# A clustered attention with a max-out feed-forward: the second copy of k's high part made by a DMA within the same partitions instead of by ScalarE

## Chip, cores and metric

The kernel runs on one core of one Trainium2 chip. The metric is the device time of one execution in microseconds (us); the median of three timed runs before the change is 864.36 us (862.89 to 865.15). A profiled execution is a run of its own, with a time of its own.

## What is computed

Attention over 4 batches, 8 heads, 768 tokens and a head dimension of 64, in which a query sees the keys of its own cluster alone, followed by a feed-forward block that takes the maximum of three products.

```python
q_assign = argmax(einsum('bhsd,hcd->bhsc', q_n, c_n), axis=-1)   # 16 clusters
k_assign = argmax(einsum('bhsd,hcd->bhsc', k_n, c_n), axis=-1)
mask = q_assign[:, :, :, None] == k_assign[:, :, None, :]
scores = scale * matmul(q, k.transpose(0, 1, 3, 2))
scores = where(mask, scores, -1e9)
attn = softmax(scores)
x = matmul(attn, v)            # to [3072 tokens, 512]
h = maximum(maximum(x @ w1, x @ w2), x @ w3)     # 512 -> 768
out = h @ w_out                                  # 768 -> 512
```

## The kernel before

**Staging of q and k.** The host hands over q and k of one head side by side, so that a tile `x` of 128 partitions has q's 64 dimensions in partitions 0 to 63 ("up") and k's in 64 to 127 ("dn"), with 768 tokens along the row. Products are made nearly exact by splitting each number into a high part that TensorE's fp32r format holds and a low remainder. For two heads (a pair) there is one tile `qk` of 128 partitions with four slots, `AQ, BQ, BK, AK`, of 2 x 768 numbers each:

- line 363 (ScalarE) writes the high parts of q and k into BQ; line 366 (GpSimd, at a few places VectorE) writes the low parts, `x - BQ`, into AQ.
- `qk_moves` (lines 369 to 376) then brings the parts where the products need them: line 373 (ScalarE) writes the scaled high part of k into AK up; line 374 (ScalarE) writes the same into BK up; line 375 (a DMA) copies k's low part from AQ dn to AK dn; line 376 (GpSimd) overwrites AQ dn with the scaled high part of q, for which line 375 must have read AQ dn.
- the cluster scores (lines 401 to 408, TensorE) and `cluster_rows` (lines 419 to 457, VectorE and GpSimd) yield one-hot rows, and line 452 (four small DMAs) puts them in partitions 64 to 79 of BQ and BK. Where a pair is prepared a second time, line 394 reads them back from a copy in DRAM.

The first pair of the first batch has its own, faster path (`first_k_moves`, lines 379 to 385). All others, 16 calls, go through `qk_moves`. One tile is prepared while the one before is in use (two buffers).

**A step of the attention.** There are 192 steps (4 batches x 8 heads x 6 blocks of 128 queries). In each, line 478 multiplies AQ with AK (128 rows: low q with high k, high q with low k), line 480 adds BQ with BK (80 rows: high with high, and the mask rows) in one of three PSUM buffers `big`. Line 483 (VectorE) takes the row maximum, line 486 (ScalarE) the exponential and its row sum, lines 487 and 488 the reciprocal. The result is normed and split into two halves of fp16, `hl` (three buffers), in one of two ways that a table `BY_POOL` chooses: lines 496 (ScalarE) and 497 (VectorE), in 147 steps, or lines 492 and 494 (GpSimd) with 493 (ScalarE), in 45. Line 498 has a DMA transpose `hl` into `pt`. For each three steps of two heads, line 510 multiplies `pt` with v.

**Around it.** Weights are loaded (line 192) and split (lines 194 to 207) during the first third. The feed-forward block of a batch (lines 545 to 590) is spread over the steps of the next one, and that of the last half batch stands at the end.

**What sets the order.** Each piece of work has a priority by the step at which it is due, and a scheduler sets the order in which each engine's instructions stand; so an edit at one place can reorder work elsewhere. All DMAs are issued by SP, in order: an issue that waits for data holds back all that stand behind it.

Of the kernel before, what the change touches and what calls it, by code (L numbers as in the profile page):

```python
# [14 lines left out]
AF = mybir.ActivationFunctionType  # L15
# [8 lines left out]
def kernel(  # L24
# [23 lines left out]
    nc = tc.nc  # L48
# [296 lines left out]
    AQ, BQ, BK, AK = range(4)  # L345
    SCALE = 1.0 / D**0.5
# [22 lines left out]
    def qk_moves(b, pr):  # L369
        t = qkt[b, pr]  # L370
        x = t.bitcast(F32)
        up, dn = slice(0, D), slice(D, 2 * D)
        nc.scalar.activation(t[up, AK], x[dn, BQ], AF.Copy, scale=SCALE)
        nc.scalar.activation(t[up, BK], x[dn, BQ], AF.Copy, scale=SCALE)
        nc.sync.dma_start(out=x[dn, AK], in_=x[dn, AQ])
        nc.gpsimd.tensor_scalar(t[dn, AQ], x[up, BQ], SCALE, 1.0, op0=ALU.mult, op1=ALU.mult)

# [81 lines left out]
    def prep_units(b, pr, pool, again=False):  # L459
        u = [lambda i=i: qk_prep(b, pr, i, pool, again) for i in range(2)]  # L460
        if again:
            f = [qk_moves, qk_masks, v_prep]
        else:
            f = [cluster_scores, qk_moves, cluster_rows] + [v_prep] * (b > 0)
        u += [lambda g=g: g(b, pr) for g in f]
        return u
# [222 lines left out]
    for b in range(B):  # L689
# [3 lines left out]
        if b:  # L693
            visits += [(b, pr, tuple(range(NG))) for pr in range(NPAIR)]
            for pr in range(NPAIR):
                if (b, pr) > (1, 0):
                    t = at + pr * 2 * V
# [60 lines left out]
```

## Time and profile before

| | |
|---|---|
| median of three timed runs | 864.36 us |
| the profiled execution, its own time | 869.48 us |
| its span, first to last instruction | 867.7 us |
| busy TensorE / VectorE / ScalarE / GpSimd | 724.6 / 604.0 / 515.3 / 487.0 us |
| mean granted TensorE clock | 0.927 |
| DMAs of line 375 | 16, each 384 KB, median 4.6 us from issue to landing |
| transposes of line 498 | 192, median 4.1 us from issue to landing |
| DMA queue of SP | 130.22 MB, 72.0% of the time of 16 engines |

The profile gives busy time per engine and, for the idle time in front of an instruction, the engine and line that ended it. "PE" is TensorE's matmuls, "PEld" its weight loads, "DVE" VectorE, "ACT" ScalarE, "POOL" GpSimd, "SPq" the DMA issues. The chain of waits starts at the last instruction and goes back, at each step to what released it.

### The profile page before, as it was taken

The page shows a single profiled execution, that of the slowest core. Times are in us where ns is not written, and L with a number is a line of the kernel's source. Part 1 is how long each engine was busy: PE and PEld are TensorE (multiplying, and loading weights), DVE is VectorE, ACT ScalarE, POOL GpSimd, SP SyncE. Part 2 cuts the span into 40 slices and gives each one's busy share as a digit, 9 for nine tenths or more (in the row PEclk, how much of TensorE's full clock was granted, in tenths as well). Part 3 has the DMA queues.
Part 4 walks back from the last instruction along what each step waited for, and adds up shares of the span by engine and source line. Part 5 has one row for each costly group of instructions (what it writes and reads, how often), then busy time and mean ns, then how long its engine had stood idle before and what let it go on. Part 6 is the DMA issues. An engine that isn't in the chain of part 4 may idle for free.

```text
span 867.7 us, 12613 instructions
## 1 busy us (share of the span) xinstructions
PE 724.6 (84%) x4220; PEld 447.9 (52%) x4220; DVE 604.0 (70%) x1135; ACT 515.3 (59%) x843; POOL 487.0 (56%) x470
## 2 busy tenths in 40 slices
PE   3534676686877999797989897979999999999997
PEld 2322444354554566464656564645655566556463
DVE  7888977978989868886769775856777677511020
ACT  7674566856957576768676756566766676510101
POOL 4695673655874467667756464746565655312111
PEclk9999666878896999989899998989999999999999
DMA  6765888999968879789798888789797865810000
GB/s 219 202 153 131 175 148 184 212 216 234 230 127 161 186 126 238 150 164 212 130 185 154 181 174 154 133 151 199 125 178 123 171 127 110 154 47 1 37 1 37
DMA packets 327680, 131.02 MB, mean 151 GB/s; under 512 B 304192, under 2 KB 313408, under 8 KB 327616
## 3 DMA queue, kind: packets, MB, share of 16 engines
q1 hardware_dynamic: 327616, 130.22, 72.0%
q8 instruction: 33, 0.54, 0.3%
q14 instruction: 31, 0.25, 0.1%
HBM read 38.57 MB, written 7.08 MB: 53 GB/s over the span
## 4 chain that ended last, share of the span: by engine, by line
PE 28%; DMA 7%; DVE 7%; ACT 5%; POOL 5%; issue 4%; SPq 0%; POOLq 0%; ACTq 0%; DVEq 0%
PE one L545 14%; DMA pt<-hl 6%; PE one L579 6%; PE one L510 3%; POOL hl L494 2%; DVE hl L497 2%; DVE nm L483 2%; PE big L478 2%; ACT hl L496 2%; ACT e L486 2%; PE big L480 1%; DMA stage<-in_v_dram 1%; POOL e L492 1%; DVE onehot L438 1%; ACT qk L363 1%
## 5 line engine op out<-in xcount | busy, mean ns | idle before, releaser
L486 ACT ACTIVATE e<-big,nm 128x768 f32<-128x768 f32 x192 | 171.6, 895 | 109.6 <-DVE nm L483 51.5
L497 DVE SCALAR_TENSOR_TENSOR hl<-e,r,hl 128x768 f16<-128x768 f32 x147 | 196.8, 1345 | 52.7 <-ACT hl L496 46.2
L545 PE MATMUL one<-x,w16a 128*128 128x384 f16 x1152 | 207.4, 336 | 5.5 <-ACT wf_h L555 3.8
L483 DVE TENSOR_REDUCE nm<-big 128x1 f32<-128x768 f32 x192 | 178.6, 946 | 11.8 <-PE big L480 11.2
L478 PE MATMUL big<-qk 128*128 128x512 f32 (+1 forms) x384 | 129.0, 419 | 68.9 <-ACT e L486 54.4
L496 ACT ACTIVATE hl<-e,r 128x768 f16<-128x768 f32 x147 | 136.1, 932 | 76.5 <-DMA pt<-hl 61.9
L545 PEld LDWEIGHTS <-w16a 128*128 128x128 f16 x1152 | 111.2, 100 | 89.1 <-issue 24.4
L510 PE MATMUL one<-pt,v 128*64 128x384 f16 x1152 | 114.8, 350 | 15.2 <-DMA pt<-hl 11.0
L480 PE MATMUL big<-qk 80*128 80x512 f32 (+1 forms) x384 | 114.8, 381 | 13.7 <-DMA qk<-cl_t 11.4
L478 PEld LDWEIGHTS big<-qk 128*128 128x128 f32 x384 | 69.3, 213 | 101.8 <-ACT e L486 71.5
L545 PE MATMUL one<-x,w16b 128*128 128x384 f16 x576 | 104.9, 338 | 7.3 <-DVE vf_h L557 5.9
L510 PEld LDWEIGHTS <-v 128*64 128x64 f16 x1152 | 73.4, 117 | 52.6 <-issue 24.7
L366 POOL TENSOR_TENSOR qk<-stage,qk 128x768 fp32r<-128x768 f32 x32 | 65.1, 2052 | 54.2 <-ACT qk L363 50.8
L494 POOL TENSOR_TENSOR hl<-e,hl 128x768 f16<-128x768 f32 x45 | 76.5, 1707 | 20.7 <-ACT hl L493 17.7
L480 PEld LDWEIGHTS big<-qk 80*128 80x128 f32 x384 | 68.8, 216 | 26.3 <-issue 8.8
L545 PEld LDWEIGHTS <-w16b 128*128 128x128 f16 x576 | 56.3, 101 | 49.6 <-issue 17.9
L487 DVE TENSOR_SCALAR r<-r 128x1 f32<-128x1 f32 x192 | 27.5, 144 | 49.2 <-ACT e L486 48.8
L492 POOL TENSOR_SCALAR e<-e,r 128x768 f32<-128x768 f32 x45 | 45.3, 1009 | 23.9 <-DVE r L488 20.9
L557 DVE SCALAR_TENSOR_TENSOR wf_h<-one,wf_h 128x384 f32<-128x384 f32 x48 | 26.5, 552 | 46.3 <-PE one L545 46.0
L557 DVE SCALAR_TENSOR_TENSOR vf_h<-one,vf_h 128x384 f32<-128x384 f32 x48 | 26.4, 550 | 46.2 <-PE one L545 46.2
L563 POOL TENSOR_SCALAR wf_h<-wf_h 128x384 f16<-128x384 f32 x24 | 16.2, 676 | 69.3 <-DVE wf_h L557 55.0
L579 PE MATMUL one<-wo,vf_h 128*128 128x512 f16 x216 | 50.2, 389 | 0.8 <-ACT o L588 0.8
(128 smaller groups left out, 934.7 us busy)
## 6 DMA issues: line engine op xcount, KB each, us to landing
stage<-in_qk_dram SPq DMA_DIRECT2D x36, 384.0 KB, 4.1
stage<-in_v_dram SPq DMA_DIRECT2D x25, 384.0 KB, 4.4
wd<-in_moe_w_dram SPq DMA_DIRECT2D x18, 512.0 KB, 4.6
qk<-qk SPq DMA_DIRECT2D x16, 384.0 KB, 4.6
out_dram<-o SPq DMA_DIRECT2D x24, 256.0 KB, 2.7
pt<-hl SPq DMA_TRANSPOSE x192, 4.1
wd<-in_moe_w_out_dram SPq DMA_DIRECT2D x6, 512.0 KB, 4.8
qk<-cl_t SPq DMA_DIRECT2D x56, 48.0 KB, 2.1
```

Source lines behind the costliest of these rows:

```text
L366: last["lo"] = eng.tensor_tensor(t[:, AQ, i], x, t[:, BQ, i].bitcast(F32), op=ALU.subtract)
L478: nc.tensor.matmul(t[:, lo:hi], aq[:, qs], ak[:, lo:hi], start=True, stop=False)
L480: last["pe"] = nc.tensor.matmul(t[:, lo:hi], bq[0:K2, qs], bk[0:K2, lo:hi], start=False, stop=True)
L483: last["nm"] = nc.vector.tensor_reduce(nm, e, axis=AX.X, op=ALU.max, negate=True)
L486: nc.scalar.activation(x, e, AF.Exp, bias=nm, scale=1.0, accum_out=r)
L492: nc.gpsimd.tensor_scalar(x, x, r, 1.0, op0=ALU.mult, op1=ALU.mult)
L494: nc.gpsimd.tensor_tensor(hl[:, 1, :], x, hl[:, 0, :], op=ALU.subtract)
L496: nc.scalar.activation(hl[:, 0, :], x, AF.Copy, scale=r)
L497: nc.vector.scalar_tensor_tensor(hl[:, 1, :], x, r, hl[:, 0, :], op0=ALU.mult, op1=ALU.subtract)
L510: nc.tensor.matmul(t[D * i : D * i + D, 0:NB], v[:, i, kt, va], pt[i][:, :, pa * QT + kt, :], start=(n == 0), stop=(n == len(todo) - 1),)
L545: nc.tensor.matmul(t[:, 0:NB], w16[jt // JA][:, jt % JA, wa, i, ct], x16[b, gi, ct][:, xa, :], start=(n == 0), stop=(n == 3 * CT - 1),)
L579: nc.tensor.matmul(t[:, 0:DM], h16[jt][:, ha, tt * P : (tt + 1) * P], wo16[0][:, jt, wa, :], start=(n == 0), stop=(n == 3 * JT - 1),)
```

## The change

Line 374 no longer computes. In its place SP issues a DMA that copies AK up, which line 373 has just written, to BK up: 64 partitions, 2 x 768 fp32 each, source and destination in the same partitions.

```diff
 def qk_moves(b, pr):
     t = qkt[b, pr]
     x = t.bitcast(F32)
     up, dn = slice(0, D), slice(D, 2 * D)
     nc.scalar.activation(t[up, AK], x[dn, BQ], AF.Copy, scale=SCALE)
-    nc.scalar.activation(t[up, BK], x[dn, BQ], AF.Copy, scale=SCALE)
+    nc.sync.dma_start(out=x[up, BK], in_=x[up, AK])
     nc.sync.dma_start(out=x[dn, AK], in_=x[dn, AQ])
     nc.gpsimd.tensor_scalar(t[dn, AQ], x[up, BQ], SCALE, 1.0, op0=ALU.mult, op1=ALU.mult)
```

The scheduler sets the order of all engines anew. At three places it reads as follows.

ScalarE, at the preparation of the second pair of the third batch (the tenth of the 16 calls); before:

```order
L363 CAST qk<-stage 128x768 x2
L496 ACTIVATE hl<-e,r 128x768
L373 ACTIVATE qk<-qk 64x1536
L374 ACTIVATE qk<-qk 64x1536
L496 ACTIVATE hl<-e,r 128x768
L486 ACTIVATE e,r<-big,nm 128x768
```

and now:

```order
L363 CAST qk<-stage 128x768 x2
L496 ACTIVATE hl<-e,r 128x768
L373 ACTIVATE qk<-qk 64x1536
L496 ACTIVATE hl<-e,r 128x768
L486 ACTIVATE e,r<-big,nm 128x768
L496 ACTIVATE hl<-e,r 128x768
```

One instruction is gone, and the rest keeps its order here.

SP's queue at the same call; before:

```order
L330 DMA stage<-in_v_dram 128x768
L498 DMA_TRANSPOSE pt<-hl 128x12x128
L375 DMA qk<-qk 64x1536
L353 DMA stage<-in_qk_dram 128x768
L498 DMA_TRANSPOSE pt<-hl 128x12x128 x2
L353 DMA stage<-in_qk_dram 128x768
L498 DMA_TRANSPOSE pt<-hl 128x12x128 x5
L452 DMA qk<-cl_t 16x768 x4
```

and now:

```order
L330 DMA stage<-in_v_dram 128x768
L498 DMA_TRANSPOSE pt<-hl 128x12x128
L374 DMA qk<-qk 64x1536
L375 DMA qk<-qk 64x1536
L498 DMA_TRANSPOSE pt<-hl 128x12x128 x3
L353 DMA stage<-in_qk_dram 128x768 x2
L498 DMA_TRANSPOSE pt<-hl 128x12x128 x3
L452 DMA qk<-cl_t 16x768 x4
```

The new DMA stands right ahead of line 375, and the two loads of the next q and k come behind three transposes. In 13 of the 16 calls the new DMA is ahead of line 375, in three behind it.

GpSimd, at the first two of the 16 calls, near the start of the program; before:

```order
L448 TENSOR_SCALAR qk<-cl_t 16x768 x2
L376 TENSOR_SCALAR qk<-qk 64x1536
L366 TENSOR_TENSOR qk<-stage,qk 128x768 x2
L430 TENSOR_TENSOR cl_t<-cl_t 128x24x16
L492 TENSOR_SCALAR e<-e,r 128x768
```

and now:

```order
L448 TENSOR_SCALAR qk<-cl_t 16x768 x2
L366 TENSOR_TENSOR qk<-stage,qk 128x768
L376 TENSOR_SCALAR qk<-qk 64x1536
L430 TENSOR_TENSOR cl_t<-cl_t 128x24x16
L366 TENSOR_TENSOR qk<-stage,qk 128x768
L492 TENSOR_SCALAR e<-e,r 128x768
```

Line 376, which waits for the DMA of line 375, has moved behind the first low part of the next pair.

## The prediction

> **What bounds the kernel now.** I read the busy time by stretches first, then the chain of waits that ended last, then the waits by engine, and last the places where the moved copy stands. In the stretches the columns are length, then busy time of PE, PEld, DVE, ACT and POOL with instruction counts, the granted TensorE clock, the DMA share and GB/s.
>
> ```profile
> 0.00:300.00 300.00, 197.18 (x952) 125.11 (x953) 256.36 (x476) 197.64 (x316) 192.63 (x203) 0.85 0.83 186
> 300.00:768.00 468.00, 433.28 (x2729) 270.00 (x2727) 334.21 (x636) 307.41 (x508) 275.89 (x241) 0.96 0.80 158
> 768.00:867.00 99.00, 94.13 (x544) 52.76 (x540) 13.38 (x24) 10.27 (x19) 18.47 (x26) 1.00 0.04 17
> ```
>
> There are three regimes. Up to 300 us VectorE is the fullest engine (256.36 of 300 us, 85%) and the DMA engines are 83% busy. From 300 to 768 us TensorE works 433.28 of 468 us, so at most 34.7 us of its idle time can be won there. The last 99 us are matmuls of the last feed-forward block, which the edit does not touch. ScalarE, from which work is taken, is 66% busy in both of the first two stretches; the DMA engines, to which it goes, are over 80% busy in them. The chain says what ended last (here the page's shares by engine and by line; "DMA pt<-hl" is the transposes of line 498):
>
> ```profile
> PE 28%; DMA 7%; DVE 7%; ACT 5%; POOL 5%; issue 4%; SPq 0%; POOLq 0%; ACTq 0%; DVEq 0%
> 368.51 1.01 PE big L478 x2
> 401.39 1.47 ACT qk L374
> 543.29 6.56 DMA pt<-hl
> 583.86 1.47 ACT qk L374
> 630.32 7.26 DMA pt<-hl
> ```
>
> The chain could be followed back to 368.51 us, so its shares add up to 56% of the span. ScalarE and DMA both stand on it, DMA a little more (7% against 5%). No engine is the bound by itself: the steps hand over to each other, and each hand-over has a few us of slack.
>
> **The change part by part.** It removes one ScalarE instruction and adds one DMA in each of the 16 calls of `qk_moves`. These are the removed instruction and its nearest relative among the DMAs, line 375, which moves the same 64 x 1536 fp32 between two slots of the same partitions, in the other half.
>
> ```profile
> L374 ACT ACTIVATE qk<-qk x16: 1464/1466/1468, 18.4 to 673.7; 64x1536 fp32r<-64x1536 f32 x16
> L375 SPq DMA_DIRECT2D qk<-qk x16: 477/512/1052, 20.2 to 673.3; - x16
> DMA to landing us min/median/max: 3.7/4.6/7.2
> ```
>
> *Removed:* 16 x 1.466 = 23.5 us of ScalarE. How much of it was on the path? Around 401 us ScalarE runs without a gap, and TensorE is the one that waits for it (the number in brackets is idle time before the instruction, and who ended it):
>
> ```profile
> 400.00 1.48 ACT L373 ACTIVATE qk<-qk 64x1536 fp32r<-64x1536 f32 x1
> 401.39 1.47 ACT L374 ACTIVATE qk<-qk 64x1536 fp32r<-64x1536 f32 x1
> 402.89 0.93 ACT L496 ACTIVATE hl<-e,r 128x768 f16<-128x768 f32 x1
> 403.73 0.88 ACT L486 ACTIVATE e<-big,nm 128x768 f32<-128x768 f32 x1
> 328.76 0.62 PE L478 MATMUL big<-qk 128*128 128x512 f32 x2 [0.48 <-ACT e L486]
> 368.51 1.01 PE L478 MATMUL big<-qk 128*128 128x512 f32 x2 [1.49 <-ACT e L486]
> 404.75 0.62 PE L478 MATMUL big<-qk 128*128 128x512 f32 x2 [1.33 <-ACT e L486]
> 493.68 0.62 PE L478 MATMUL big<-qk 128*128 128x512 f32 x2 [1.48 <-ACT e L486]
> ```
>
> Line 486 empties the PSUM buffer that the next scores need, and lines 373 and 374 push it back. Four of the 16 calls (the last four rows, each within 5 us of a line 374) end in such a stall: 0.48 + 1.49 + 1.33 + 1.48 = 4.8 us. The chain gives a second reading: of the seven calls after 368.51 us two have their line 374 on it, so 16 x 2/7 x 1.466 = 6.7 us. The bounds are 0 and 23.5 us; I take **-6.7 us**, the reading by the chain, because the cost below can be read in the same way.
>
> *Added:* 16 transfers of 384 KB on the one SP queue. What one occupies is read from a stretch of 5.4 us (582.6 to 588.0 us) that holds just two DMAs of 384 KB; here packets, MB and share of the 16 engines, then the two issues with the time to landing:
>
> ```profile
> q1 hardware_dynamic: 224, 0.79, 59.1%
> qk<-qk SPq DMA_DIRECT2D x1, 384.0 KB, 3.7
> stage<-in_v_dram SPq DMA_DIRECT2D x1, 384.0 KB, 4.6
> ```
>
> 59.1% of 5.4 us is 3.2 us, so 1.6 us each if they share it equally (an estimate), and 25.6 us for 16, about as much as ScalarE is relieved of. The copy has 64 partitions; the Trainium skill, "SBUF — State Buffer", section "Door 1: The DMA port swizzle", says that partitions 0 to 63 reach 8 of 16 ports and gives about 218 GB/s for them, which speaks against the change: 1.8 us instead of the 0.9 us that all 16 ports would give. By it (an estimate) the next term would be 8.2 us instead of 7.3 us; the 1.6 us above is the trace's version.
>
> The reader of the copy, line 480, does not feel it: it also needs the mask rows of line 452, which stand behind the copy on the same queue with transposes between (or, where a pair is prepared again, the mask of line 394 behind it), so they land later. What feels it is what is queued behind, above all the transposes, since ScalarE may not write a new `hl` before an old one has been transposed:
>
> ```profile
> ACT hl L496 <- DMA pt<-hl: 61.9, 42, 7.0
> POOL qk L376 <- DMA qk<-qk: 13.6, 4, 5.4
> 179.06 0.93 ACT L496 ACTIVATE hl<-e,r 128x768 f16<-128x768 f32 x1 [6.29 <-DMA pt<-hl]
> 680.26 0.94 ACT L496 ACTIVATE hl<-e,r 128x768 f16<-128x768 f32 x1 [1.14 <-DMA pt<-hl]
> ```
>
> After 6 of the 16 present copies of line 375, ScalarE stands in such a wait within 9 us (the last two rows are the first and the last of the six). On the chain it is 2 of 7; SP's own rows show the copies ahead of the two chain pieces of 543.29 and 630.32 us:
>
> ```profile
> 538.87 1.00 SPq L375 DMA_DIRECT2D qk<-qk  x1
> 540.60 5.85 SPq L498 DMA_TRANSPOSE pt<-hl  x2
> 629.08 0.50 SPq L375 DMA_DIRECT2D qk<-qk  x1
> 630.32 2.76 SPq L498 DMA_TRANSPOSE pt<-hl  x1
> ```
>
> The transpose on the chain is the second behind the copy there and the first here. With 1.6 us more ahead of them, 16 x 2/7 x 1.6 = **+7.3 us**. The bounds: 0, if each copy falls into free DMA time, and 16 x (1.6 + 0.5) = 33.6 us, if every one with its 0.512 us of issue delays the path.
>
> *Moved:* SP runs in order. The new issue waits for line 373 where line 375 waits for GpSimd's line 366. In 12 of the 16 calls of before line 373 had ended when line 375 was issued; in the other four it ended later, the most in this call:
>
> ```profile
> 582.47 1.48 ACT L373 ACTIVATE qk<-qk 64x1536 fp32r<-64x1536 f32 x1
> 582.66 0.50 SPq L375 DMA_DIRECT2D qk<-qk  x1
> ```
>
> That is 1.3 us after the issue, so the queue is held little longer than now. But in 13 of the 16 pairs of the new order the new DMA stands ahead of line 375, whose landing moves back by 1.6 + 0.5 = 2.1 us. Line 376 on GpSimd waits for that landing (it overwrites what line 375 reads), and did so four times for 13.6 us in all. Four times 2.1 us is 8.4 us of GpSimd; with GpSimd's part of the chain, 5 of 56, that is **+0.8 us** (bounds 0 and 8.4). What stands behind line 376 on GpSimd in the new order is line 430 (cluster scores), 334 or 207 (scaling v, splitting weights), on which the next scores do not wait at once.
>
> *Sum:* -6.7 + 7.3 + 0.8 = +1.4 us. The profiled execution took 869.48 us (its span of 867.7 and 1.8 around it), 5.1 us above the median of the timed runs, 864.36 us. The terms are differences within that execution, so I lay them on the median: **865.8 us**.
>
> **The rivals.** *Relief without a price (faster).* If the DMA engines' free 17 to 20% takes up the copies, only the first term stays: 864.4 - 6.7 = 857.7 us. For it speaks that ScalarE is backed up after most calls; against it that 6 of 16 present copies are followed by a wait for transposes.
>
> *Transposes set ScalarE's pace (slower).* At the six places ScalarE saves 1.47 us and then waits up to 2.1 us longer, because with three `hl` buffers it cannot run ahead. Then the relief is worth nothing there and the six waits count in full: 6 x 2.1 = 12.6 us, 864.4 + 12.6 = 877.0 us; with the issue hidden and the GpSimd term, 6 x 1.6 + 0.8, it is 874.8 us. It decides from the point where the transpose in flight is the oldest of three: the 42 waits of before show that this is so at 42 of the 147 uses of line 496.
>
> *The new order meets other locks (either sign).* The edit makes the scheduler set the order anew on all engines, and one kind of stall depends on chance meetings:
>
> ```profile
> 60.02 7.93 DVE L497 SCALAR_TENSOR_TENSOR hl<-e,r,hl 128x768 f16<-128x768 f32 x1
> 62.18 1.62 POOL L494 TENSOR_TENSOR hl<-e,hl 128x768 f16<-128x768 f32 x1
> 63.77 3.36 POOL L207 TENSOR_TENSOR w16a<-wf,w16a 128x512 f16<-128x512 f32 x3
> 86.91 6.18 DVE L497 SCALAR_TENSOR_TENSOR hl<-e,r,hl 128x768 f16<-128x768 f32 x1 [1.66 <-ACT hl L496]
> L497 DVE SCALAR_TENSOR_TENSOR hl<-e,r,hl x147: 975/1019/7933, 34.7 to 752.7; 128x768 f16<-128x768 f32 x147
> ```
>
> Line 497 takes 1.02 us, but 7.93 and 6.18 us here, while GpSimd runs instructions end to end: 6.9 and 5.2 us lost. If one such stall goes, the sum becomes 864.4 + 1.4 - 6.9 = 858.9 us; if one more comes, 872.7 us. The Trainium skill, "SBUF — State Buffer", section "SBUF: two separate sides", says that a VectorE instruction with two SBUF inputs and a GpSimd instruction exclude each other for the whole instruction of the one that came first. One such instruction, at most 1.6 us in the rows above, would be the price by it; the trace shows that a row of them can be.
>
> That the copy does not do what it says is no rival worth a chance: the same 64 x 1536 values arrive, and the order has 16 new DMAs and 16 fewer ScalarE instructions.
>
> **How the numbers follow.** About what a measurement of this kernel can tell from no change is 0.3%, 2.6 us. The balanced sum gets 0.36; its own range is 861.8 to 867.0 us, which is "same". Transposes that set the pace get 0.28, and a new stall 0.10: slower 0.38. Relief without a price gets 0.14 and a stall that goes 0.12: faster 0.26. The range reaches down below 857.7 us, to 855, since the first term is bounded by 23.5 and not 6.7 us, and up to 876, past 874.8 us and just short of the worst count.
>
> **What would show it.** Line 374 gone from ScalarE and 32 DMAs qk<-qk; the queue's share of 16 engines up from 72.0 to about 75%. First term right: TensorE's stalls on line 486 behind line 373 shrink by about 1.4 us each. Second right: the wait of line 496 for transposes grows from 61.9 us by some 10 us. Third right: the wait of line 376 for line 375 grows from 13.6 towards 22 us. I am wrong if the stretch up to 300 us alone moves by more than 5 us with these waits unchanged; then the order did it.

## The result, and the profile after

The changed kernel takes 876.09 us (median of 22 runs, 868.81 to 885.95), the kernel before 865.9 us (22 runs, 860.82 to 872.95). The ratio is 1.0097, 95% interval 1.0076 to 1.0119: slower by 1.0%, some 8.4 us. It leaves out the four slowest runs of the changed kernel (882.51 us and above), which lie over 1.5% above its fastest; with them it would be 1.012.

The two profiled executions hardly differ (868.81 us after, 869.48 us before): that of after is the fastest of its 22 runs, that of before lies 3.6 us above its median. So the spans say nothing here, and the waits have to be compared. First the stretches of after, with the columns of the prediction:

```profile
0.00:300.00 300.00, 192.78 (x982) 125.78 (x983) 265.55 (x480) 191.40 (x314) 197.31 (x206) 0.86 0.87 194
300.00:768.00 468.00, 424.29 (x2707) 266.22 (x2706) 336.96 (x632) 292.64 (x496) 269.78 (x240) 0.97 0.84 165
```

ScalarE has 6.2 and 14.8 us less work in them, and the DMA engines are fuller by four points in both (up from 0.83 and 0.80 to 0.87 and 0.84). The page of after shows this by queue and by DMA, and the trace the landing of the new transfers alone (line 374):

```profile
q1 hardware_dynamic: 328896, 136.52, 75.8%
...
qk<-qk SPq DMA_DIRECT2D x32, 384.0 KB, 5.2
...
pt<-hl SPq DMA_TRANSPOSE x192, 4.1
```
```profile
DMA to landing us min/median/max: 4.0/4.6/7.5
```

The median transpose lands as before, after 4.1 us. What counts is the few that somebody stands and waits for. These are waits of before that the prediction does not show, and then the waits of after (us in total, times, longest):

```profile
PE big L478 <- ACT e L486: 54.4, 34, 9.2
...
DVE hl L497 <- ACT hl L496: 46.2, 41, 5.8
```

```profile
ACT hl L496 <- DMA pt<-hl: 85.4, 46, 6.3
DVE hl L497 <- ACT hl L496: 64.7, 52, 6.3
...
PE big L478 <- ACT e L486: 49.4, 32, 9.1
...
POOL qk L376 <- DMA qk<-qk: 11.7, 3, 6.0
```

ScalarE was relieved of 21.5 us (busy 515.3 us before, 493.8 after), and its wait for transposes grew from 61.9 to 85.4 us, by 23.5. ScalarE now stands about as long at the transposes as it was relieved. VectorE, which waits for ScalarE in line 497, goes from 46.2 to 64.7 us, and TensorE's wait for line 486, which the relief was to shorten, falls by 5.0 us only. On the chain the DMA engines' share has grown, while ScalarE's is 5% as before (the page's shares, then two pieces of the chain):

```profile
PE 26%; DMA 12%; DVE 9%; ACT 5%; POOL 4%; issue 4%; SPq 2%; ACTq 0%; POOLq 0%; DVEq 0%
```
```profile
323.73 6.76 DMA pt<-hl
...
395.35 5.77 DMA pt<-hl
```

DMA had 7% of the span on the chain before and has 12% now. The chain of after could be followed back a little further, to 323.73 us, so that its shares add up to 62% in place of 56%; of what could be followed, DMA has 19% in place of 12%.

### The profile page after: what moved, and what is told of

The parts are those of the page before. It is cut to its first block, busy times and chain, and to the rows that moved or that the text cites. A ratio compares the mean times of both kernels' runs of the same rounds, so it can differ in the third digit from the quotient of the medians.

```text
span 867.0 us, 12641 instructions
## 1 busy us (share of the span) xinstructions
PE 710.1 (82%) x4220; PEld 444.1 (51%) x4220; DVE 615.9 (71%) x1135; ACT 493.8 (57%) x827; POOL 485.3 (56%) x470
## 3 DMA queue, kind: packets, MB, share of 16 engines
q1 hardware_dynamic: 328896, 136.52, 75.8%
## 4 chain that ended last, share of the span: by engine, by line
PE 26%; DMA 12%; DVE 9%; ACT 5%; POOL 4%; issue 4%; SPq 2%; ACTq 0%; POOLq 0%; DVEq 0%
PE one L545 14%; DMA pt<-hl 11%; PE one L579 6%; PE one L510 4%; DVE hl L497 3%; DVE nm L483 2%; ACT hl L496 2%; PE big L478 2%; ACT e L486 1%; PE big L480 1%; POOL hl L494 1%; SPq L498 1%; DMA stage<-in_v_dram 1%; POOL e L492 1%; DVE cl_t L436 1%
## 5 line engine op out<-in xcount | busy, mean ns | idle before, releaser
L497 DVE SCALAR_TENSOR_TENSOR hl<-e,r,hl 128x768 f16<-128x768 f32 x147 | 198.0, 1352 | 70.1 <-ACT hl L496 64.7
L545 PE MATMUL one<-x,w16a 128*128 128x384 f16 x1152 | 202.8, 332 | 8.7 <-DVE r L487 3.6
L496 ACT ACTIVATE hl<-e,r 128x768 f16<-128x768 f32 x147 | 136.1, 932 | 109.4 <-DMA pt<-hl 85.4
L478 PE MATMUL big<-qk 128*128 128x512 f32 (+1 forms) x384 | 127.4, 414 | 61.2 <-ACT e L486 49.4
L510 PE MATMUL one<-pt,v 128*64 128x384 f16 x1152 | 115.7, 353 | 23.5 <-DMA pt<-hl 12.2
L545 PE MATMUL one<-x,w16b 128*128 128x384 f16 x576 | 100.2, 329 | 6.7 <-DVE vf_h L557 2.9
L494 POOL TENSOR_TENSOR hl<-e,hl 128x768 f16<-128x768 f32 x45 | 76.1, 1697 | 14.8 <-ACT hl L493 11.8
L480 PEld LDWEIGHTS big<-qk 80*128 80x128 f32 x384 | 68.7, 216 | 25.8 <-issue 13.2
L493 ACT CAST hl<-e 128x768 f16<-128x768 f32 x45 | 37.2, 828 | 34.9 <-POOL e L492 31.3
L579 PE MATMUL one<-wo,wf_h 128*128 128x512 f16 x216 | 52.0, 398 | 1.7 <-ACT o L588 0.8
L563 POOL TENSOR_SCALAR wf_h<-wf_h 128x384 f16<-128x384 f32 x24 | 15.7, 656 | 63.2 <-DVE wf_h L557 57.1
```

The source lines that it names most:

```text
L478: nc.tensor.matmul(t[:, lo:hi], aq[:, qs], ak[:, lo:hi], start=True, stop=False)
L480: last["pe"] = nc.tensor.matmul(t[:, lo:hi], bq[0:K2, qs], bk[0:K2, lo:hi], start=False, stop=True)
L494: nc.gpsimd.tensor_tensor(hl[:, 1, :], x, hl[:, 0, :], op=ALU.subtract)
L496: nc.scalar.activation(hl[:, 0, :], x, AF.Copy, scale=r)
L497: nc.vector.scalar_tensor_tensor(hl[:, 1, :], x, r, hl[:, 0, :], op0=ALU.mult, op1=ALU.subtract)
L510: nc.tensor.matmul(t[D * i : D * i + D, 0:NB], v[:, i, kt, va], pt[i][:, :, pa * QT + kt, :], start=(n == 0), stop=(n == len(todo) - 1),)
```

## The experiments

The edit changes two things at once: the work of one instruction, and, through the scheduler, the order of instructions on every engine. To part them, most kernels below have the order of each engine written out as a table, so that only the named instruction differs. In the traces every engine, the DMA queue included, has the order that is named for it. The table itself costs nothing that can be seen: with it, experiments 1, 3, 9 and 11 run within 0.3% of before. Each ratio is to the kernel before on the same chip (medians 866.1 to 867.7 us), 5 rounds each, with its 95% interval.

**1. The order alone.** Line 374 stays on ScalarE; all other instructions stand in the order of the changed kernel.

```diff
  # every engine in the order of the changed kernel
- nc.sync.dma_start(out=x[up, BK], in_=x[up, AK])
+ nc.scalar.activation(t[up, BK], x[dn, BQ], AF.Copy, scale=SCALE)
```

> Line 374 on ScalarE again, right behind line 373, no new DMA, but every engine held to the order that the changed kernel has. 'Price': ratio to before 0.996 to 1.004. 'Order': 1.006 to 1.015, at least as slow as the changed kernel, since the 23.5 us of ScalarE come back on top.

Measured: 866.27 us, 0.9996 (0.9964 to 1.0028). The new order costs nothing by itself. Its waits are a second "before" for the changed kernel, with the same order:

```profile
ACT hl L496 <- DMA pt<-hl: 63.8, 41, 4.6
DVE hl L497 <- ACT hl L496: 60.8, 56, 5.2
...
PE big L478 <- ACT e L486: 50.3, 29, 8.6
```

Against these, the edit adds 21.6 us to the wait of line 496 (63.8 to 85.4), while VectorE's 60.8 us were mostly there already: part of the growth in line 497's wait belongs to the order. The 1.0% comes with the edit itself, not with the order.

**2. The transfer alone, in the order of before.** Line 374 as a DMA, right ahead of line 375's.

```diff
  # every engine in the order of before
- nc.scalar.activation(t[up, BK], x[dn, BQ], AF.Copy, scale=SCALE)
+ nc.sync.dma_start(out=x[up, BK], in_=x[up, AK])
```

> The DMA in place of ScalarE's line 374, but every engine held to the order that it had before the change; the new DMA stands right ahead of line 375 on SP. Theory 'price' (the transfers delay the transposes behind them, order is innocent): as slow as the change itself, ratio to before 1.006 to 1.013, and line 496's wait for transposes 75 to 95 us against 61.9. Rival 'order' (the scheduler's new order is what costs): ratio 0.993 to 1.002, since only relief and a hidden transfer are left. Rival 'relief wins in the old order': ratio under 0.993.

Measured: 886.41 us, 1.0209 (1.0157 to 1.0261). In the order of before the edit costs twice as much, 18 us. Waits of this kernel, and then two of before that have not been shown yet:

```profile
ACT hl L496 <- DMA pt<-hl: 73.8, 43, 7.7
PE big L478 <- ACT e L486: 66.0, 37, 10.0
...
POOL qk L376 <- DMA qk<-qk: 25.1, 4, 9.5
POOL stage L334 <- DMA stage<-in_v_dram: 24.6, 9, 6.5
...
ACT v L338 <- POOL stage L334: 19.9, 7, 5.5
```
```profile
POOL stage L334 <- DMA stage<-in_v_dram: 11.8, 7, 3.3
...
ACT v L338 <- POOL stage L334: 5.5, 6, 1.6
```

The first three waits have grown, by 11.9, 11.6 and 11.5 us. The last two belong to the preparation of v: line 330 loads it, GpSimd scales it in line 334, and ScalarE makes its fp16 half in line 338. GpSimd waits 12.8 us longer for the load, and ScalarE 14.4 us longer for GpSimd. Which wait the end follows is asked in experiments 4 to 6, and again behind the dose. The work itself has not become slower: one line 496 takes 0.932 us and one line 483 0.945 us here and in experiment 3 alike.

**3. The relief alone.** ScalarE's line 374 is taken out and nothing is put in its place.

```diff
  # every engine in the order of before
- nc.scalar.activation(t[up, BK], x[dn, BQ], AF.Copy, scale=SCALE)
...
- aq, bq, bk, ak = (qkt[b, h // 2][:, j, h & 1] for j in range(4))
+ aq, bq, bk, ak = (qkt[b, h // 2][:, j, h & 1] for j in (AQ, BQ, AK, AK))
```

> The order of before held, line 374 left out and nothing in its place; line 480 reads slot AK instead of BK, so BK's mask rows and BK's copy of k take no part in the scores. It shows what 23.5 us of ScalarE are worth alone. By the forecast's first term 6.7 us, ratio about 0.992; if ScalarE is never the one that ends last, 0.998 to 1.002; if all of it counted, 0.973.

Measured: 865.68 us, 0.9976 (0.9945 to 1.0007). 23.5 us less of ScalarE are worth some 2 us, perhaps none. Waits of this kernel:

```profile
ACT hl L496 <- DMA pt<-hl: 68.6, 45, 6.4
...
ACT e L486 <- DVE hl L497: 35.2, 20, 6.7
...
POOL stage L334 <- DMA stage<-in_v_dram: 15.6, 8, 3.6
...
ACT v L338 <- POOL stage L334: 10.2, 7, 3.0
```

Even with no transfer added, ScalarE's wait for transposes grows from 61.9 to 68.6 us. That is only a part of the relief: the wait ahead of line 486 that ends with VectorE's line 497 grows from 25.8 to 35.2 us, and line 338's wait for v from 5.5 to 10.2 us. Freed of line 374, ScalarE mostly comes earlier to points where it must wait.

**4. The reader taken away.** As 2, but nobody reads what the transfer brings.

```diff
  # as experiment 2, and
- aq, bq, bk, ak = (qkt[b, h // 2][:, j, h & 1] for j in range(4))
+ aq, bq, bk, ak = (qkt[b, h // 2][:, j, h & 1] for j in (AQ, BQ, AK, AK))
```

> The new transfer in the order of before, ahead of line 375's as in dma_old_order (1.0209), but nobody reads what it brings: line 480 reads the first copy (AK) in place of the second (BK), so its mask rows and the second copy take no part in the result. Theory A, the 16 engines (the transfer takes their time, and transposes and loads land later): as dma_old_order, 1.016 to 1.026, some 883 us. Theory B, SyncE's queue in order (the issue waits for ScalarE's line 373 and holds what is queued behind it): the same, 1.016 to 1.026. Theory C, the readers (TensorE's line 480 waits for a copy that lands some 4 us after ScalarE's own would have been there): the price is gone, 0.996 to 1.003, as relief_old_order (0.9976).

Measured: 889.09 us, 1.023 (1.0174 to 1.0286). The price is all there without a reader, so line 480's wait for the copy is not it.

**5. SyncE's queue taken away.** The same transfer from ScalarE's own queue, at the place where the copy stood.

```diff
  # every engine in the order of before
- nc.scalar.activation(t[up, BK], x[dn, BQ], AF.Copy, scale=SCALE)
+ nc.scalar.dma_start(out=x[up, BK], in_=x[up, AK])
```

> The same transfer issued from ScalarE's own queue, at the very place where line 374's copy stood, every engine in the order of before: SyncE's queue is that of before. Theory A, the 16 engines: the bytes are the same, so 1.012 to 1.026. Theory B, SyncE's queue: nothing new stands in it, so the price is gone; ScalarE pays an issue of some 0.5 us in place of 1.47 us: 0.996 to 1.004. Theory C, the readers: the copy lands some 3 us earlier than from SyncE's queue, so a part of the price, 1.004 to 1.014.

Measured: 885.68 us, 1.0242 (1.0187 to 1.0297). SyncE's queue is that of before, and the price is the same; an issue that waits in order and holds up others is not it. Nor is the granted clock, which over the runs is 0.902 in the mean here and 0.903 in those of before beside them. The page now shows the 16 transfers by themselves, as queue q10:

```profile
q1 hardware_dynamic: 327616, 130.22, 71.3%
q10 hardware_dynamic: 1280, 6.29, 3.5%
```

3.5% of the span of 884.5 us is 31.0 us of each of the 16 DMA engines on average, 1.9 us for one transfer.

**6. Behind line 375 in place of ahead of it.**

```diff
  # every engine in the order of before
+ nc.sync.dma_start(out=x[dn, AK], in_=x[dn, AQ])
  nc.sync.dma_start(out=x[up, BK], in_=x[up, AK])
- nc.sync.dma_start(out=x[dn, AK], in_=x[dn, AQ])
```

> As dma_old_order, but the new transfer stands right behind line 375's in SyncE's queue, not ahead of it. Theory A, the 16 engines: little changes, since both transfers go out together, 1.014 to 1.026; if what matters is that line 376 waits for line 375's transfer and 1.8 us of the engines less stand ahead of it, the wait of line 376 falls back from 25.1 to about 14 us and the ratio to 1.010. Theory B, SyncE's queue: line 375 no longer waits behind a wait, what follows still does: 1.008 to 1.016. Theory C, the readers: line 480's copy lands later still, 1.020 to 1.030.

Measured: 887.19 us, 1.0227 (1.0183 to 1.0271). Two of its waits:

```profile
ACT hl L496 <- DMA pt<-hl: 79.7, 46, 7.6
...
POOL qk L376 <- DMA qk<-qk: 14.4, 4, 7.1
```

Line 376's wait is back from 25.1 to 14.4 us (before: 13.6), and the time stays. So GpSimd's wait for line 375 is not the price either; what has gone up further is the wait for transposes, to 79.7 us, and line 338's wait for v stays long, at 19.9 us.

**7. Later.** The transfer is held back until just ahead of the mask rows of line 452, mostly some 20 us after line 375's.

```diff
  # order of before; in SyncE's queue now
+ nc.sync.dma_start(out=x[up, BK], in_=x[up, AK])   # line 374
  nc.sync.dma_start(out=x[D:D+C, BQ+(g>>1), g&1], in_=ttf[32*g:32*g+C, :])   # line 452
```

> As dma_old_order, but the new DMA stands later on SP, right ahead of the mask rows of its pair (line 452 or 394), behind the transposes that are queued there. 'Price by queue place' (it costs because it stands ahead of line 375, of line 376's wait and of the transposes that ScalarE needs just then): faster than dma_old_order by 0.4% or more. 'Price by occupation' (any 384 KB on the 16 engines costs the same): within 0.2% of dma_old_order.

Measured: 877.26 us, 1.0125 (1.0076 to 1.0175), against 1.0209 right beside line 375. The two intervals just overlap; by the ratios some 40% of the price hangs on the moment, and away from line 375's transfer and the loads behind it the same transfer costs less.

**8 and 9. The dose.** As experiment 4, with half the bytes and with almost none.

```diff
  # as experiment 4, but
- nc.sync.dma_start(out=x[up, BK], in_=x[up, AK])
+ nc.sync.dma_start(out=x[up, BK, 0], in_=x[up, AK, 0])                          # 8: half
+ nc.sync.dma_start(out=x[0:16, BK, 0, 0:128], in_=x[0:16, AK, 0, 0:128])        # 9: tiny
```

> As dma_unread (the order of before, ScalarE's line 374 gone, the new transfer ahead of line 375's and nobody reads it, line 480 reads AK; 1.023), but the transfer carries only the first head of the two: 64 packets of 3072 bytes in place of 6144, half the time of the engines. Theory A, the engines' time: between relief_old_order (0.998) and dma_unread (1.023), 1.006 to 1.016. Theory D, the number of transfers (one more completion that something behind it has to wait for, whatever its size): the whole price, 1.018 to 1.026. Theory E, a threshold (only what goes beyond the gap in the queue costs): near nothing, 0.996 to 1.005.

Measured: 871.18 us, 1.0049 (1.0021 to 1.0077): just below what theory A gives, and inside the range of theory E, the threshold.

> As half_unread, but the transfer carries 16 packets of 512 bytes, under one per cent of the bytes, at the same place in SyncE's queue and with the same waits. Theory A, the engines' time: the price is gone, 0.995 to 1.003, as relief_old_order. Theory D, the number of transfers or their place in the queue: 1.015 to 1.026.

Measured: 868.89 us, 1.0017 (0.999 to 1.0044). A transfer without weight costs at most a little: its ratio lies 0.4% above that of experiment 3 (0.9976), and the intervals overlap. So it is in the main the bytes, not the number of transfers. But the price is not even: from no transfer to half it is 0.73%, 6.3 us; from half to whole 1.8%, 15.7 us.

The traces show the wait for transposes at one instruction that all these kernels have in the same order: the line 496 ahead of step 86 of the 192, behind one of the preparations. Here it stands in the timelines of before, of experiment 3 (no transfer), 9 (tiny), 8 (half), 5 (ScalarE's queue) and 6 (behind line 375), one fence each; in brackets the wait ahead of it:

```profile
373.27 0.94 ACT L496 ACTIVATE hl<-e,r 128x768 f16<-128x768 f32 x1 [1.90 <-DMA pt<-hl]
```
```profile
376.81 0.93 ACT L496 ACTIVATE hl<-e,r 128x768 f16<-128x768 f32 x1 [4.66 <-DMA pt<-hl]
```
```profile
376.47 0.93 ACT L496 ACTIVATE hl<-e,r 128x768 f16<-128x768 f32 x1 [5.03 <-DMA pt<-hl]
```
```profile
375.83 0.93 ACT L496 ACTIVATE hl<-e,r 128x768 f16<-128x768 f32 x1 [5.58 <-DMA pt<-hl]
```
```profile
382.40 0.93 ACT L496 ACTIVATE hl<-e,r 128x768 f16<-128x768 f32 x1 [6.79 <-DMA pt<-hl]
```
```profile
387.06 0.94 ACT L496 ACTIVATE hl<-e,r 128x768 f16<-128x768 f32 x1 [7.61 <-DMA pt<-hl]
```

First line to second: ScalarE's 1.47 us gone, and the wait longer by 2.76 us; the relief is swallowed on the spot, and why the transpose lands 1.3 us later still is not shown. From the second on, the wait is longer by up to 2.95 us, with a transfer that stands ahead of the transposes on the 16 engines. (In experiments 2 and 4, with the whole transfer, it is 5.43 and 5.67 us here, about as with half; their loss stands at other places. So this is one place in single executions, not a measure of the price.)

Summed over the span, the wait for transposes is not all of the price, nor the part that follows the dose best. In the order of before, line 338's wait for v is 10.2 us without a transfer (3), 14.1 with the tiny one (9), 12.7 with half (8), and 19.9, 20.5, 19.2 and 19.9 us with the whole one (2, 4, 5, 6). Line 496's wait for transposes is 68.6, 68.6 and 65.2 us, and then 73.8, 70.3, 75.8 and 79.7 us. With the transfer held back (7) the two are 12.3 and 70.1 us, nearly as without it. The source is visible at the five loads of v that are issued within 1 us behind line 375: they land after 4.4 to 5.2 us in experiment 3, and after 6.1 to 7.9 us in experiment 4. So by these waits the loads of v behind the transfer weigh about as much in this order as the transposes. In the changed kernel's own order it is mostly the transposes: from experiment 1 to it their wait grows by 21.6 us and line 338's by 3.5. No run moves the loads of v alone, so how many microseconds of the end belong to each stays open.

**10. The same question from the other side.** Line 374 stays on ScalarE. Line 375's transfer is taken out with nothing in its place.

```diff
  # every engine in the order of before
- nc.sync.dma_start(out=x[dn, AK], in_=x[dn, AQ])
...
- aq, bq, bk, ak = (qkt[b, h // 2][:, j, h & 1] for j in range(4))
+ aq, bq, bk, ak = (qkt[b, h // 2][:, j, h & 1] for j in (AQ, BQ, BK, AQ))
```

> Before, held in its order, without line 375's transfers and with nothing in their place: line 478 reads AQ in place of AK on k's side, so line 375's copy takes no part. It says what one transfer of this size is worth when it is taken away, and with line375_by_gpsimd (1.0001) what GpSimd's copy costs. Theory A with an even price (each transfer costs some 1.2 us, the first as the second): 0.975 to 0.985 (846 to 855 us), and GpSimd's 23.5 us cost as much as the transfers. Theory E, a threshold (the transfers of before fit into the gaps and only the added ones stand in the way): 0.993 to 1.001, and GpSimd's copy costs nothing either.

Measured: 847.03 us, 0.9777 (0.9745 to 0.9808). The gain of 19 us is what an even price gives, and speaks against a threshold that only added transfers cross. This kernel loses more than the transfer, though: lines 478 and 376 no longer wait for any copy, and a part of the gain is no matter of transfers, as experiments 11 and 12 show.

**11 and 12. An engine in place of line 375's transfer.** If the transfer is dear and an engine's time cheap, this should win: GpSimd right ahead of line 376, or ScalarE behind line 374, where by the trace of before the input is ready.

```diff
  # every engine in the order of before
- nc.sync.dma_start(out=x[dn, AK], in_=x[dn, AQ])
+ nc.gpsimd.tensor_scalar(t[dn, AK], x[dn, AQ], 1.0, 1.0, op0=ALU.mult, op1=ALU.mult)   # 11
+ nc.scalar.copy(t[dn, AK], x[dn, AQ])                                                  # 12
```

> The test from the other side: before is kept with line 374 on ScalarE, and line 375's transfer (the other one, as large) is replaced by a copy on GpSimd right ahead of line 376, every engine otherwise in the order of before. GpSimd is busy 16 x 1.47 = 23.5 us more, and its wait of 13.6 us for line 375's transfers goes. Theory A, the 16 engines: their share falls by 16 x 1.8 us to about 69%, and as much is gained as the added transfers cost, less what GpSimd's time costs: 0.982 to 0.994 (852 to 862 us). Theory B, SyncE's queue: one issue fewer at each place that waits for GpSimd's line 366: 0.988 to 0.998. Theory C, the readers: line 478 has its rows some 3 us earlier: 0.990 to 1.000. If GpSimd's time costs as much as the transfer did: 1.000 to 1.010.

> A version that may beat both: before, held in its order, with line 375's transfer replaced by a copy on ScalarE, placed behind line 374 at the first place where by the trace of before its input is ready (up to eight instructions later). ScalarE works 16 x 1.47 = 23.5 us more, the 16 transfers are gone. Theory A, the engines' time, with ScalarE's time as cheap as relief_old_order had it (0.24% for as many us): the gain of no_375 (0.9777) less 0.002 to 0.010, that is 0.980 to 0.988 (849 to 856 us). If an engine's copy at this place always costs what the transfer did, as GpSimd's did (1.0001): 0.997 to 1.006. If ScalarE's added time holds line 486 and so TensorE up by 1.4 us at each place, as the first step of the prediction assumed: 0.985 to 0.995.

Measured: 867.24 us, 1.0001 (0.9972 to 1.0031) with GpSimd; 867.61 us, 1.0016 (0.9996 to 1.0035) with ScalarE. Neither wins; theory A missed both. The wait for transposes did fall, here in the waits of 11 and of 12:

```profile
ACT hl L496 <- DMA pt<-hl: 51.9, 40, 6.4
```
```profile
ACT hl L496 <- DMA pt<-hl: 49.9, 38, 6.7
```

That is 10 and 12 us less than before (61.9), and it was given back. One place is visible, early in the timeline of experiment 12:

```profile
50.84 11.05 DVE L497 SCALAR_TENSOR_TENSOR hl<-e,r,hl 128x768 f16<-128x768 f32 x1
51.05 5.25 POOL L339 TENSOR_TENSOR v<-vf,v 128x384 f16<-128x384 f32 x6
56.27 0.99 POOL L430 TENSOR_TENSOR cl_t<-cl_t 128x384 f32<-128x384 f32 x1
57.23 1.63 POOL L494 TENSOR_TENSOR hl<-e,hl 128x768 f16<-128x768 f32 x1
58.82 2.25 POOL L207 TENSOR_TENSOR w16a<-wf,w16a 128x512 f16<-128x512 f32 x2
```

Line 497 takes 11.05 us in place of 1.02, as long as GpSimd runs ten instructions end to end. Experiment 11 has the same (11.20 us). In experiment 10, with the same order, no line 497 up to 70 us takes over 2.39 us. Before has its 7.93 us there. By the 13th of the 192 steps, just behind this stall, experiment 10 is 10.4 us ahead of 11 and 6.5 us ahead of 12, a third to a half of the 20 us between them. Before, too, is 8.6 us behind experiment 10 there, of the 23 us by which these two profiled executions differ at the end. So over a third of experiment 10's gain is there just behind a stall that it misses, and it is no clean price of one transfer. The rest was not taken apart.

## Why the prediction came out as it did

The range (855 to 876 us) held: the measured ratio on 864.36 us gives 872.7 us. The likeliest case, 865.8 us and no change, did not hold. The kernel went the way of the rival "Transposes set ScalarE's pace" (874.8 to 877.0 us). That the range held is in part luck: the relief was worth less and the transfer cost more than forecast, and in the order of before the same edit (1.0209 to 1.0242) gives 882 to 885 us, outside of the range. Only the new order, which softened the loss and from which the forecast expected nothing of the kind, brought it back inside.

*Removed, -6.7 us: sized too high.* ScalarE's work fell as said. Experiment 3 values it at 0.24% or 2.1 us (interval from a gain of 4.8 to a loss of 0.6). The step that failed is the reading by the chain: that line 374 stands on the chain for 1.47 us was taken to mean that 1.47 us are won when it goes. What is late next was not asked there: the transpose of an old `hl`, which ScalarE waits for 2.76 us longer at the place shown, and in other places VectorE's line 497 and v. TensorE's stalls behind line 373 did not shrink by 1.4 us each in total either: line 478's wait for line 486 is 49.4 us after, and 50.3 us in experiment 1, with line 374 on ScalarE in the same order.

*Added, +7.3 us: sized too low.* The mechanism is right in kind: the price is there without a reader (4), without SyncE's queue (5), without line 376's longer wait (6), and goes with the bytes for the most part (8, 9). In the order of before it is the step from experiment 3 to 2, 4, 5 and 6, that is 2.3 to 2.7%, 20 to 23 us or 1.3 to 1.4 us for each of the 16. The duration was near: 1.6 us estimated, 1.9 us of each engine measured on a queue of its own. By the Trainium skill, "SBUF — State Buffer", section "Door 1: The DMA port swizzle", 1.8 us came out as an estimate, and the trace, with 1.9 us, agrees with it better than with the 1.6 us. What failed is the factor 2/7: I counted only the copies whose transposes were on the chain already. 20 to 23 us are as much as 10 to 12 of 16 transfers at 1.9 us. And I priced transposes alone: the loads of v behind the copy I put at nothing, and in the held order line 338's wait for them grew by 9.0 to 10.3 us from experiment 3 to 2, 4, 5 and 6, the transposes' by 1.7 to 11.1 us. A chain names the waits that ended last today; a burden of 2 us at 16 places made others long.

*GpSimd, +0.8 us: right in kind, without weight.* Against before, line 376's wait did not grow towards 22 us but fell, from 13.6 to 11.7 us. In one and the same order it grew as said: line 376's wait for line 375 goes from 5.2 us (experiment 1) to 11.7 us with the transfer, not far from the 8.4 us worked out. But experiment 6 takes 11 us of this wait away and the time does not move.

*Moved.* The order is no cause of the loss (0.9996); it softened it. With the transfer the new order stands at 1.0097, the old one at 1.0209 to 1.0242. Experiment 7 shows that the moment of the transfer can make such a difference, but which of the moved instructions does it in the changed kernel stays open. One difference is in the waits: in the new order line 338's wait for v goes from 3.2 us (experiment 1) to 6.7 us with the edit, in the old order from 10.2 us (experiment 3) to 19.9 us (experiment 2).

*The sign that I had set for myself,* line 496's wait up by some 10 us, came out at 23.5 us. Of the waits on the list it is the one that told the outcome. The locks of line 497 did change (before 7.93 and 6.18 us, longest after 8.23 us), but experiment 1 has the new order with them and no loss.

*What stays open.* Why the first half of a transfer costs 6.3 us and the second 15.7: a slack ahead of each wait, used up by about the first microsecond, would do it, and was only argued; that line 338's wait for v grows with the second half and hardly with the first fits it. How the price divides between the loads of v and the transposes. And how the 19 us of experiment 10 divide between the DMA engines' time, the copy's latency and the stall of line 497. No complete version ran that beats both kernels; experiment 10 leaves a copy out.

## What to carry to other kernels

Before moving work off an engine, look at what that engine waits for next: an engine that waits dozens of times for transposes, loads or other engines may only wait longer when it is relieved, as here, where 23.5 us less work were worth some 2 us. A transfer within SBUF is not free because its bytes stay on the chip: it is paid in the time of the shared DMA engines, and where they are over 80% busy and others queue behind, as here, most of it can reach the end. List everything that is queued behind it, loads as well as transposes. To price such an edit, hold the order and change one instruction: a term read off the few places that are on the chain today was here too small for the added burden and too large for the removed one.

## What was not expected of the hardware

- 16 copies of 384 KB between slots of the same 64 partitions took 31.0 us of each of the 16 DMA engines on average, 1.9 us each, and cost 20 to 23 us of the kernel's time in the order of before. The same copy with half the bytes cost 6.3 us.
- The queue made no difference: from SyncE's queue 1.0209, from ScalarE's 1.0242, with overlapping intervals.
- A VectorE instruction of 1.02 us took 11.05 us while ten GpSimd instructions ran in a row, and ended 0.8 us after the last of them. The Trainium skill, "SBUF — State Buffer", section "SBUF: two separate sides", has the wait last for the instruction that came first; here it outlasted ten.
